# Seven half-size products for the output layer of groups 1 to 8, instead of groups 6 to 8 only

## The chip, the core and the metric

The kernel runs on one core of a Trainium2 chip. The metric is device time in microseconds, from the start of the program on the core to its end; lower is better. The core has five engines that run side by side, each through its own instructions in order: PE (TensorE, matrix products; its weight loads are shown as PEld), DVE (VectorE), ACT (ScalarE), POOL (GpSimd) and SP (SyncE, which here only issues DMAs). They wait for each other through semaphores.

## What is computed

Two layers in a row: linear attention with a softmax-like feature map, and a gated feed-forward layer. Batch 8, 8 heads, 576 positions, head size 64, 128 features; the feed-forward layer has 4608 tokens, a width of 512 and 1536 hidden values.

```python
def phi(x):
    proj = np.einsum('bhsd,df->bhsf', x, w_phi)
    proj = proj - np.max(np.abs(proj), axis=-1, keepdims=True)
    return np.concatenate([np.exp(proj), np.exp(-proj)], axis=-1)
q_p, k_p = phi(q), phi(k)
kv = np.einsum('bhsf,bhsd->bhfd', k_p, v)
z = np.sum(k_p, axis=2)
num = np.einsum('bhsf,bhfd->bhsd', q_p, kv)
den = np.einsum('bhsf,bhf->bhs', q_p, z)[..., None] + 1e-06
x = (num / den)             # tokens x 512 after the heads are put together
gate = np.maximum(x @ w_gate, 0.0)
val = x @ w_val
out = gate * val @ w_out
```

## The kernel before

**Groups.** The 4608 tokens are nine groups of 512. Groups 0 to 7 are the first 512 positions of each batch; group 8 holds the last 64 positions of all eight batches. A group has four blocks of 128 tokens (index t or i), and the hidden layer twelve blocks of 128 values (index f).

**An order written out.** The string ORDER lists some two thousand steps, and the kernel walks through it. A word such as `fv.1.3:0@val3` is a call of `do_fv` for group 1, block 3, on PSUM bank 0, and `@` gives the room of a ring of buffers that a new tile takes. Each engine runs its own steps in the order of this string; a step waits for the steps whose results or rooms it needs. Nothing else plans the work.

**Steps of the attention.** `kt`, `ku`, `qt` transpose k and q (DVE). `kr` (PE, L572) and `qc` (PE, L834) form the projections, `ke` and `qe` their exponentials (ACT, L668 and L849), `kx` and `qx` the maxima (DVE), `kk` the scale of k (ACT). `vs` and `vq` scale v with it (POOL, L725 and L753). `kv` is the product of features and v (PE, L774), `nu` that of q's features with it (PE, L897); `mc`, `mn` are the same for group 8. `nt`, `nv`, `nr` and `nx` normalize (DVE three times, L918, L928 and L936, then POOL, L940), and `xt` turns the result into the layout xT for the next layer with a DMA on SP's queue. `lk`, `lq`, `lm`, `ln` are loads that POOL issues, `lv` and `lw` those of SP.

**Steps of the feed-forward layer.** `fv` and `fg` are the value and gate products of one hidden block (PE, L1074, four products of 512 columns). `va` (ACT) or `vb` (DVE) copies the value from PSUM, `ga` (DVE, L1095) makes h = max(gate, 0) x value in bf16. Group 0 is done in smaller pieces (`pv`, `pg`).

**The output in groups 0 to 5.** `fo.g.t.part` is a third of out[t] = h[:, t] times w_out (PE, L1135, twelve products of 512 columns for a block t, 48 for a group). `oc` (ACT) or `oe` (DVE) copies the bank into one of three buffers ob, and `od` (SP) writes it out.

**The output in groups 6 to 8** is computed by the Winograd form of Strassen's product. h is cut in halves by tokens (r) and by hidden blocks (c), w_out by hidden blocks and by columns; seven products of half size take the place of eight, with sums around them:

- `tw.n.hf` (POOL, L1223): the four differences of blocks of w_out, once for all groups, each in two parts. They lie in the rooms of kn, qn and kT, which are free late.
- `ps.g.n.j` (POOL, L1240): the four sums of blocks of h, n = 1 to 4, for each of six hidden blocks j; 128 x 256 each. Sums 1 and 2 are followed by those that read them.
- `fw.g.n` (PE, L1264): product n, twelve products of 256 columns. Product 5 reads sum 1, 6 reads sum 2, 7 reads sum 3, 3 reads sum 4; 1, 2 and 4 read h itself.
- `ys`, `y2` (ACT) copy banks; `yw`, `yz`, `y1`, `y3`, `y4` (DVE, L1295) add banks into the output in SBUF. The last four quarters come out of these.
- `ow`, `oq` (SP) and `oz` (ACT's queue) write out. `ow` of group 8 is two DMAs, since its blocks hold two batches.

The sums take rooms of the ring vs (four), h takes the ring h2 (15 rooms), and in groups 7 and 8 the rooms of kp.

Of the kernel before, what the change touches and what calls it, by code (L numbers as in the profile page):

```python
# [8 lines left out]
FP32 = mybir.dt.float32  # L9
# [67 lines left out]
fo.0.3.2:1 ln.1.1 lw.2.1 qc.2.0:2456 kt.3.0@kT3 ke.2.2.0.1:3 fv.1.3:0 kx.2.2.3:7 vs.2.0.1@vs0
qx.2.0.3:6 qx.2.0.0:2 oc.0.3:1@ob0 kk.2.1.1 fv.1.4:1 qe.2.0.1.0:4@qp2 vb.1.4:1@val0 vs.2.1.0@vs3
qe.2.0.1.1:4 ke.2.2.0.0:3 kk.2.2.0@ek1 qx.2.0.2:5 kk.2.2.1 qe.2.0.3.1:6@qp3 fg.1.3:7 qe.2.0.3.0:6
vb.1.3:0@val3 fv.1.5:3 lw.3.0 fv.1.1:1 qe.2.0.0.1:2@qp4 fv.1.6:6 qe.2.0.2.1:5@qp0 qt.2.1@qT2  # L80
fg.1.4:0 vb.1.1:1@val2 va.1.5:3@val1 qe.2.0.0.0:2 vs.2.2.1@vs1 ga.1.3:7@hs12 qx.2.0.1:4 qe.2.0.2.0:5
va.1.6:6@val3 qc.2.1:3215 ga.1.4:0@hs13 mn.0.1:7 qe.2.1.2.1:1 fg.1.6:4 ku.3 qe.2.1.3.1:5 qx.2.1.1:2
qe.2.1.0.0:3 fv.1.8:6 nt.8.0.1:7@t1 vs.2.1.1 qx.2.1.3:5 qe.2.1.2.0:1 fg.1.5:0 qx.2.1.0:3
qe.2.1.3.0:5 qx.2.1.2:1 qe.2.1.1.0:2 fv.1.10:5 vq.2.1 qe.2.1.0.1:3 ga.1.5:0@hs14 va.1.8:6@val0
fg.1.0:1 nv.8.0.1:7 vs.2.0.0 lw.3.1 va.1.10:5@val1 ga.1.6:4@hs0 od.0.2 qe.2.1.1.1:2 kr.3.0:3076
lm.4.1 fv.1.0:5 kx.3.0.0:3@mk3 ke.3.0.2.1:7@kp2 lq.3.2 ke.3.0.3.1:6 kx.3.0.1:0 qy.2.0:4 ke.3.0.0.0:3
fg.1.8:2 qz.2.0:4@my0 ke.3.0.1.1:0 vs.2.2.0 kt.3.1@kT2 va.1.0:5@val3 kv.2.0:4 kx.3.0.2:7
ke.3.0.1.0:0 kv.2.1:5 ke.3.0.0.1:3 qu.2.0@mz1 ga.1.8:2@hs1 lm.4.0 lv.3.1 qw.2.0@cq0 ke.3.0.3.0:6
# [48 lines left out]
nt.8.1.0:1@t2 qe.4.0.1.0:4 qc.4.1:5732 kd.4.1:0@kv1 vs.4.2.0 fo.2.1.0:6 qe.4.1.0.1:5 qx.4.1.3:2
# [129 lines left out]
def kernel(  # L267
# [11 lines left out]
    nc = tc.nc  # L279
# [1093 lines left out]
```

## Time and profile before

| | us |
|---|---|
| median of 3 runs | 371.83 (371.48 to 373.03) |
| the profiled execution's own time | 371.23 |
| its span (first to last instruction) | 369.4 |
| HBM read / written | 37.81 MB / 9.44 MB |

The granted clock of TensorE is full speed in every slice of the span. "Busy" is the union of the intervals in which an engine had an instruction; short overlaps of neighbours count once. "x48" is a number of instructions. The chain of work that ended last is followed back from the last instruction, at each step to what released it. In stretches, the columns are the length, then for PE, PEld, DVE, ACT and POOL the busy time and the number of instructions, then the clock, the DMA share and GB/s. Lines L... are lines of the kernel. In the groups, out<-in stands for the tile written and those read, and the numbers behind the bar are the busy time in us and the mean of one in ns, then the idle time of the engine ahead of it with what ended it.

### The profile page before, as it was taken

The numbers are of one execution on the slowest core, as the hardware profiler recorded it, in microseconds if no ns is written. First come the engines' busy times: TensorE is split into PE (matmuls) and PEld (weight loads), VectorE is DVE, ScalarE is ACT, GpSimd is POOL, SyncE is SP. The second block draws the span as 40 slices with busy tenths as digits, with TensorE's granted clock in tenths as the row PEclk, the third lists the DMA queues.
The fourth block names the chain that finished last, engine by engine and source line by source line (L and its number), as shares of the span: only waits on it lengthen the run. The fifth ranks groups of instructions, "written<-read, shape, count | busy, mean of one in ns | idle before, by whom it ended". The sixth has DMA issues, their size and how long they took to land.

```text
span 369.4 us, 9471 instructions
## 1 busy us (share of the span) xinstructions
PE 359.6 (97%) x3672; PEld 206.1 (56%) x3720; DVE 292.9 (79%) x682; ACT 228.1 (62%) x552; POOL 215.1 (58%) x241
## 2 busy tenths in 40 slices
PE   8999999999999999999999999999999999999995
PEld 6579865446544654464465444654445684444674
DVE  6999999999989999999888797777558775347433
ACT  4999996998588855986775539735656402312110
POOL 8675995293379049713760438367078972285690
PEclk9999999999999999999999999999999999999999
DMA  8999999909657983493356061835020010700007
GB/s 132 248 206 196 174 196 144 184 26 164 108 127 113 170 135 76 71 186 78 80 114 105 14 116 57 138 83 118 0 59 1 2 27 14 232 0 3 0 18 212
DMA packets 90767, 38.13 MB, mean 103 GB/s; under 512 B 64226, under 2 KB 86370, under 8 KB 90722
## 3 DMA queue, kind: packets, MB, share of 16 engines
q0 software_dynamic: 33504, 15.03, 30.9%
q1 hardware_dynamic: 57074, 22.36, 26.6%
q8 instruction: 29, 0.48, 0.5%
q14 instruction: 16, 0.13, 0.1%
q10 hardware_dynamic: 144, 0.13, 0.1%
HBM read 37.81 MB, written 9.44 MB: 128 GB/s over the span
## 4 chain that ended last, share of the span: by engine, by line
PE 82%; POOL 7%; DVE 5%; DMA 3%; issue 2%; ACT 0%; POOLq 0%; DVEq 0%
PE bank L1074 42%; PE bank L1135 16%; PE bank L1264 6%; PE bank L774 4%; PE bank L1103 4%; POOL vs L1240 4%; PE bank L897 4%; DMA vn<-in_v_dram 3%; PE bank L572 2%; PE bank L834 2%; DVE h L1095 2%; DVE mk L676 1%; POOL vs L725 1%; DVE t L918 1%; PE bank L1053 1%
## 5 line engine op out<-in xcount | busy, mean ns | idle before, releaser
L668 ACT ACTIVATE kp<-bank 128x384 bf16<-128x384 f32 x192 | 84.4, 517 | 20.0 <-PE bank L572 13.1
L1089 ACT CAST val<-bank 128x512 bf16<-128x512 f32 x81 | 47.2, 595 | 65.3 <-PE bank L1074 44.4
L1074 PE MATMUL bank<-xTs,wv 128*128 128x512 bf16 x338 | 86.0, 379 | 0.7
L1074 PE MATMUL bank<-xTs,wg 128*128 128x512 bf16 x335 | 85.2, 379 | 0.9
L940 POOL TENSOR_TENSOR xu<-u,r 128x512 bf16<-128x512 f32 x36 | 37.3, 1042 | 71.6 <-DVE r L936 51.6
L849 ACT ACTIVATE qp<-bank 128x512 bf16<-128x512 f32 x128 | 70.0, 621 | 11.6 <-PE bank L834 9.9
L1135 PE MATMUL bank<-wo,h 128*128 128x512 bf16 x274 | 66.1, 379 | 0.7 <-issue 0.2
L725 POOL TENSOR_TENSOR vs<-vn,ek 128x780 bf16<-128x780 f32 (+2 forms) x40 | 53.7, 1365 | 21.4 <-ACT ek L685 13.5
L1074 PEld LDWEIGHTS <-wg 128*128 128x128 bf16 x400 | 37.5, 98 | 40.7
L1095 DVE SCALAR_TENSOR_TENSOR h<-bank,val 128x512 bf16<-128x512 f32 x76 | 51.0, 679 | 11.5 <-PE bank L1074 8.8
L1074 PEld LDWEIGHTS <-wv 128*128 128x128 bf16 x400 | 37.1, 98 | 41.2 <-issue 1.5
L676 DVE TENSOR_REDUCE mk<-bank 128x3 f32<-128x384 f32 x96 | 50.1, 541 | 5.3 <-ACT kp L668 3.3
L1135 PEld LDWEIGHTS <-h 128*128 128x128 bf16 x288 | 26.4, 98 | 31.2 <-issue 2.4
L857 DVE TRANSPOSE_TENSOR_REDUCE maxq<-bank 128x16 f32<-128x512 f32 x56 | 37.2, 691 | 3.9 <-ACT qp L849 2.0
L928 DVE TENSOR_TENSOR u<-bank,t 128x195 f32<-128x195 f32 (+1 forms) x108 | 33.5, 329 | 3.0 <-POOL xu L940 1.2
L918 DVE TENSOR_TENSOR t<-bank,cq 128x195 f32<-128x195 f32 (+1 forms) x96 | 30.0, 325 | 3.3 <-PE bank L897 3.1
L897 PEld LDWEIGHTS <-qp 128*128 128x128 bf16 x512 | 23.0, 98 | 11.2 <-issue 1.9
L1095 DVE SCALAR_TENSOR_TENSOR kp<-bank,val 128x512 bf16<-128x512 f32 x24 | 16.1, 688 | 14.9 <-PE bank L1074 13.1
L897 PE MATMUL bank<-kv,qp 128*128 128x65 bf16 x512 | 25.8, 193 | 0.3 <-ACT kv L785 0.2
L774 PEld LDWEIGHTS <-kp 128*128 128x128 bf16 x640 | 21.5, 97 | 3.2 <-issue 0.7
L774 PE MATMUL bank<-vs,kp 128*128 128x65 bf16 x512 | 22.1, 193 | 0.4 <-POOL vs L725 0.4
L753 POOL TENSOR_TENSOR vr<-vm,ek 64x520 bf16<-64x520 f32 x14 | 14.8, 1060 | 11.0 <-DMA vm<-in_v_dram 9.6
(129 smaller groups left out, 492.7 us busy)
## 6 DMA issues: line engine op xcount, KB each, us to landing
vn<-in_v_dram SPq DMA_DIRECT2D x24, 256.0 KB, 4.9
out_dram<-ob SPq DMA_DIRECT2D x24, 256.0 KB, 3.1
kn<-in_k_dram POOLq DMA_DIRECT2D x7, 512.0 KB, 9.5
qn<-in_q_dram POOLq DMA_DIRECT2D x7, 512.0 KB, 7.5
wv<-in_moe_w_val_dram POOLq DMA_DIRECT2D x3, 512.0 KB, 9.6
wg<-in_moe_w_gate_dram POOLq DMA_DIRECT2D x3, 512.0 KB, 9.1
wo<-in_moe_w_out_dram POOLq DMA_DIRECT2D x3, 512.0 KB, 8.1
out_dram<-xTs SPq DMA_DIRECT2D x5, 256.0 KB, 2.6
```

What stands on the lines that cost most here:

```text
L668: nc.scalar.activation(kp_of(3 * b + j)[:, i, s].rearrange("p n f -> p (n f)"), bank[bk[0]][:, 0 : 3 * F], AF.Exp, scale=(1.0, -1.0)[s],)
L676: nc.vector.tensor_reduce(mk_of(3 * b + j)[:, :, i], bank[bk[0]][:, 0 : 3 * F].rearrange("p (n f) -> p n f", f=F), axis=AX.X, op=ALU.max, ...
L725: nc.gpsimd.tensor_tensor(vs_of(3 * b + j)[:, s, 0:n].rearrange("p n i e -> p (n i) e")[:, :, 0:e], src[:, lo:hi].rearrange("p h i e -> p ...
L774: nc.tensor.matmul(out_ps[:, h - lo, s, :], lhsT=lhsT, rhs=rhs, start=(at == 0), stop=(at == 2 * n * (C + 1) - 1),)
L849: nc.scalar.activation(qp_of(4 * b + i)[:, s, 4 * hq : 4 * hq + 4].rearrange("p h m -> p (h m)"), bank[bk[0]], AF.Exp, scale=(1.0, -1.0)[s],)
L857: nc.vector.tensor_reduce((maxq0[:, i] if b == 0 else maxq)[:, :, i, 4 * hq : 4 * hq + 4].rearrange("p t h -> p h t"), bank[bk[0]].rearran ...
L897: nc.tensor.matmul(bank[bk[0]][:, E * n : E * (n + 1)], lhsT=qp_of(4 * b + i)[:, s, h, :], rhs=kv_of(b)[:, h, s, 0:E],)
L940: eng.tensor_tensor(xu_of(n).rearrange("p (h d) -> p h d", d=D), u_of(n)[:, :, 0:D], r_of(n).to_broadcast([P, H, D]), op=ALU.mult,)
L1074: nc.tensor.matmul(bank[bk[0]], lhsT=w[:, dc, P * f : P * f + P], rhs=xT(g)[:, dc, :], start=(dc == 0), stop=(dc == NDC - 1),)
L1089: nc.scalar.copy(val_of(NFC * g + f), bank[bk[0]])
L1095: nc.vector.scalar_tensor_tensor(h2_of(g, f), bank[bk[0]], 0.0, val_of(NFC * g + f), op0=ALU.max, op1=ALU.mult)
L1135: nc.tensor.matmul(bank[bk[0]], lhsT=h2_of(g, f)[:, P * t : P * t + P], rhs=wo_sb[:, f, :], start=(f == 0), stop=(f == NFC - 1),)
```

## The change

- Groups 1 to 5 take the seven half-size products as well. Their `fo`, `oc`, `oe` and `od` words are gone; `fw`, `ps`, `ys`, `y...` and `ow` words stand in their place. Group 0 keeps `fo`, and all its four copies are `oc` on ACT.
- The three ob buffers become one pair. Group 0's four output blocks have four rooms: two in its own xT room and the pair. In later groups the first half of the output goes into the group's own xT room and the second into the pair (group 7: the xT room of group 6).
- The differences of w_out are made early, right after group 0's output, and stay: the first in place over the block of w_out that no later product reads, the second and third in room kp3, the fourth in room qp0. So kp has three rooms and qp four for the rest.
- Sums 3 and 4 of h are written over the blocks of h that they replace. vs has five rooms, h2 sixteen; group 8's h lies in h2.
- 18 sums, 12 of group 7 and 6 of group 8, are made by DVE (new step `ds`, function of the same formula) instead of POOL.
- From the word `oc.0.1` on the whole of ORDER is in another sequence. Ahead of it nothing differs.

```diff
-    vs_of = ring("vs", 4, [P, 2, 3, 4, EP], BF16)
+    vs_of = ring("vs", 5, [P, 2, 3, 4, EP], BF16)
-    ob_of = ring("ob", 3, [P, DM], FP32)
+    ob_pair = sb.tile([P, 2, DM], FP32, name="obp", tag="obp")
-    NH2 = 15
+    NH2 = 16
...
     def do_oc(bk, g, t):
-        nc.scalar.copy(ob_of(4 * g + t), bank[bk[0]])
+        nc.scalar.copy(ow_pair(g, t // 2)[:, t % 2], bank[bk[0]])
...
-    WG = (6, 8, 7)
+    WG = tuple(range(1, B + 1))
...
+    def tw_all(n):
+
+        if n == 0:
+            return wo_sb[:, 0:HK, HN:DM]
+        if n == 3:
+            return flat_of(qp_of(("tw",)).rearrange("p s h m -> p (s h m)"), HK)
+        t = kp_of(("tw",)).rearrange("p i s n f -> p (i s n f)")
+        return flat_of(t[:, HK * HN * (n - 1) : HK * HN * n], HK)
...
-    def sum_of(g, n):
+    def sum_of(g, n, j):
+
+        if n > 2:
+            return h_block(g, 1, 0, j) if n == 3 else h_block(g, 0, 1, j)
         t = vs_of(("sum", g, n)).rearrange("p s n i e -> p (s n i e)")
-        return flat_of(t, HK)
+        return flat_of(t, HK)[:, j]
...
     def ow_pair(g, r):
 
-        room = {6: (xT_all[:, 0], xT_all[:, 1]), 8: (xT_all[:, 0], xT_all[:, 1])}.get(
-            g, (xT_all[:, 2], xT_mix)
-        )[r]
+        if r == 1 and g != B - 1:
+            return ob_pair
+        room = xT(g) if r == 0 else xT_all[:, 2]
```

Of the new sequence, two stretches of which the prediction speaks: the one around group 2's first kv, with the differences of w_out in front, and the end.

```
oc.0.0:4 kr.2.2:3054 ku.3@kT3 qt.2.0@qT0 xt.1.1 ke.2.1.0.1:7 xt.1.0 tw.1.0 ke.2.1.3.0:6 ln.1.1
...
ke.2.2.0.1:3 kk.2.0.0 qc.2.0:6401 fv.1.3:2 fv.1.10:3 od.0.1 oc.0.3:7 tw.0.0 qe.2.0.1.0:4@qp2 tw.0.1
...
qc.2.1:7650 od.0.2 qe.2.1.2.0:5 fg.1.6:1 qe.2.1.0.0:7 va.1.11:2@val3 qx.2.1.1:6 fg.1.11:4 vs.2.1.0
kt.3.0 qx.2.1.0:7 kv.2.1:3 vs.2.2.0@vs0 qe.2.1.1.1:6 qe.2.1.0.1:7 qt.3.1@qT1 vs.2.2.1 od.0.3 tw.2.1
...
ds.7.4.3 y1.7.1:5 fw.8.4:1 y3.8:1 ow.8.2 ow.8.3 ps.8.4.2 ds.7.4.4 ps.8.4.4 fw.7.5.0:2 ps.8.4.3
ps.8.4.0 fw.7.4:3 y1.7.0:2 oq.7.1.1 fw.8.3:0 y3.7:3 oq.7.1.0 fw.7.3.1:5 fw.7.3.0:2 y4.8:0 y4.7.1:5
y2.8:6 ow.8.0 ow.8.1 oz.7.1 y4.7.0:2 ow.7.0.1
```

The words by kind, before and after: fo 72 and 12, oc 16 and 4, oe 8 and 0, od 24 and 4, fw 23 and 58 (four of them half steps), ps 72 and 174, ds 0 and 18, ow 9 and 29, ys 3 and 8, y2 3 and 8, yw, yz and y3 3 and 8 each, y1 and y4 4 and 9 each.

More of the change, by code (lines that the diff above doesn't have):

```diff
@@ new lines @@
+qe.3.0.1.0:7 qe.3.0.2.0:4 kk.3.2.1@ek4 kk.3.0.1 fw.1.7:0 yz.1:0 ps.1.4.0 qe.3.0.3.0:2@qp4
+qc.3.1:3674 qx.3.1.3:4 qx.3.1.0:3 vs.3.1.0@vs4 ps.1.4.3 lq.4.2 xt.2.2 kk.3.2.0 vq.3.0@vr0 ps.1.4.2
+qe.3.0.3.1:2 fw.1.4:0 vq.3.1 vs.3.1.1 vs.3.2.0@vs0 qe.3.1.3.1:4 qe.3.1.3.0:4 kt.4.1@kT2 vs.3.2.1
+qe.3.1.1.1:6 fv.2.10:2 qe.3.0.0.1:1@qp1 y3.1:0 fv.2.2:4 fg.2.1:0 qx.3.1.1:6 va.2.10:2@val0
+qe.3.1.0.1:3 qe.3.1.1.0:6 fv.2.1:2 qx.3.0.0:1 qx.3.1.2:7 ps.1.4.1 fg.2.2:6 kt.4.0 vb.2.2:4@val2
+ps.1.4.5 qe.3.1.0.0:3 y1.1:5 qe.3.0.0.0:1 qy.3.0:3 qz.3.0:3@my1 kv.3.1:1 qu.3.0@mz0 fv.2.11:4
@@ new lines @@
+qt.5.1@qT0 va.3.11:6@val2 nx.4.0@xu3 nv.4.1.0:5 fv.3.10:6 fg.3.1:5 ga.3.11:7@hs9 va.3.1:2@val3
+nr.4.1@r1 nt.4.3.1:4@t2 vs.5.0.1@vs2 kx.5.1.3:0 ps.3.1.5 nt.4.3.0:3@t1 fg.3.4:7 nu.4.3.2:2
+kx.5.1.2:1 ke.5.1.2.1:1 nv.4.3.1:4@u0 ga.3.1:5@hs8 nv.4.3.0:3 va.3.10:6@val1 nt.4.3.2:2@t3
+kr.5.2:0415 xt.8.0 ga.3.4:7@hs2 nu.4.2.1:6 fv.3.7:3 ke.5.2.2.1:1@kp2 nv.4.3.2:2 nr.4.3@r2
+ke.5.2.0.0:0 fg.3.7:7 kx.5.2.2:1@mk5 nu.4.2.2:2 va.3.7:3@val2 ke.5.2.3.1:5 vq.5.1@vr0 ow.2.2
+nt.4.2.1:6@t0 fg.3.10:3 ga.3.7:7@hs0 ke.5.2.2.0:1 nx.4.1@xu0 fv.3.8:1 nt.4.2.2:2@t2 xt.4.1
@@ new lines @@
+nt.5.0.2:0@t0 kk.6.0.1 fv.4.9:3 y4.3:2 nt.5.0.1:1@t2 ow.3.3 nv.5.0.2:0 nu.5.1.2:4 fv.4.2:6
+nv.5.0.1:1 nu.5.1.0:2 nt.5.1.2:4@t1 nr.5.0@r2 vq.6.0@vr1 nx.5.0@xu3 lw.6.1 va.4.9:3@val2 fg.4.9:3
+nv.5.1.2:4@u1 nu.5.3.0:0 xt.5.0 nt.5.1.0:2@t3 nu.5.3.1:1 nt.5.3.1:1@t0 nt.5.3.0:0@t2 my.2:4
+va.4.2:6@val0 mz.2:4@my2 fg.4.4:6 ke.6.0.0.1:5 nv.5.3.0:0@u2 fv.4.0:5 ga.4.9:3@hs11 nu.5.1.1:4
+nu.5.2.0:0 ga.4.4:6@hs5 fv.4.6:3 ps.4.1.1@vs1 nt.5.2.0:0@t1 fv.4.8:6 nv.5.1.0:2 nt.5.1.1:4@t2
+nv.5.1.1:4 vb.4.0:5@val2 nu.5.3.2:2 nu.5.2.2:4 fv.4.3:5 nv.5.3.1:1 va.4.3:5@val1 nr.5.1@r1 lv.6.0
@@ new lines @@
+ke.7.2.1.1:0 fv.5.11:6 fw.5.1:2 ps.5.3.3 ke.7.2.0.0:3 ke.7.2.1.0:0 va.5.11:6@val0 ps.5.1.2
+ga.5.6:7@hs3 ke.7.2.3.0:5 kk.7.1.1@ek4 ps.5.1.1 ys.5:2 ps.5.1.0 fg.5.11:1 kx.7.2.2:4 kx.7.2.0:3
+qc.7.0:7063 xt.6.2 kx.7.2.3:5 kk.7.2.0@ek2 vq.7.0@vr0 ke.7.2.2.1:4 kk.7.1.0 ga.5.11:1@hs12
+qx.7.0.1:0 qe.7.0.1.1:0@qp4 qt.7.1@qT2 ps.5.2.0 xt.6.1 qx.7.0.2:6 fw.5.2:2 vs.7.1.1@vs2 xt.6.0
+fv.6.0:5 fg.6.0:1 va.6.0:5@val1 ga.6.0:1@hs14 qe.7.0.1.0:0 y2.5:2 fv.6.4:5 fv.6.1:0 ps.5.4.0
+va.6.4:5@val2 fv.6.10:1 ps.5.3.0 ke.7.2.2.0:4 va.6.1:0@val3 fg.6.4:2 qe.7.0.2.0:6@qp3 fv.6.3:5
@@ L1064, in h2_of @@
         i = NFC * g + f
-        if g >= B - 1:
+        if g == B - 1:
             t = kp_of(("h", g, f // 6)).rearrange("p i s n f -> p (i s n f)")
@@ L1143, in do_oc @@
     def do_oc(bk, g, t):
-        nc.scalar.copy(ob_of(4 * g + t), bank[bk[0]])
+        nc.scalar.copy(ow_pair(g, t // 2)[:, t % 2], bank[bk[0]])
     def do_oe(bk, g, t):
-        nc.vector.tensor_copy(ob_of(4 * g + t), bank[bk[0]])
+        nc.vector.tensor_copy(ow_pair(g, t // 2)[:, t % 2], bank[bk[0]])
     def do_od(bk, g, t):
@@ L1153, in do_od @@
                 dst = out[0:SF, :].rearrange("(p c) n -> p c n", c=C)[:, t]
-            nc.sync.dma_start(out=dst, in_=ob_of(4 * g + t))
+            nc.sync.dma_start(out=dst, in_=ow_pair(g, t // 2)[:, t % 2])
             return
@@ L1158, in do_od @@
             nc.sync.dma_start(
-                out=out[r0 : r0 + SM, :], in_=ob_of(4 * g + t)[SM * bb : SM * (bb + 1)]
+                out=out[r0 : r0 + SM, :], in_=ow_pair(g, t // 2)[:, t % 2][SM * bb : SM * (bb + 1)]
             )
-    HD = DM // 2
-    def do_fp(bk, g, t, half):
-        for f in range(NFC):
-            nc.tensor.matmul(
-                bank[bk[0]][:, 0:HD],
-                lhsT=h2_of(g, f)[:, P * t : P * t + P],
-                rhs=wo_sb[:, f, HD * half : HD * (half + 1)],
-                start=(f == 0),
-                stop=(f == NFC - 1),
-            )
-    def do_o1(bk, g, t):
-        nc.scalar.copy(ob_of(4 * g + t)[:, 0:HD], bank[bk[0]][:, 0:HD])
-    def do_o2(bk, g, t):
-        nc.vector.tensor_copy(ob_of(4 * g + t)[:, HD:DM], bank[bk[0]][:, 0:HD])
-    def do_d1(bk, g, t):
-        r0 = S * g + P * t
-        nc.scalar.dma_start(out=out[r0 : r0 + P, 0:HD], in_=ob_of(4 * g + t)[:, 0:HD])
-    def do_d2(bk, g, t):
-        r0 = S * g + P * t
-        nc.sync.dma_start(out=out[r0 : r0 + P, HD:DM], in_=ob_of(4 * g + t)[:, HD:DM])
-    WG = (6, 8, 7)
+    WG = tuple(range(1, B + 1))
     HK = NFC // 2
@@ L1257, in do_fw @@
                 else:
-                    x = sum_of(g, {3: 4, 5: 1, 6: 2, 7: 3}[n])[:, j]
+                    x = sum_of(g, {3: 4, 5: 1, 6: 2, 7: 3}[n], j)
                 if n in (1, 2, 3):
```

392 lines of the change are left out of this document (180 added, 212 removed).

## The prediction, made before the changed kernel was run

> **What bounds the kernel now.** I read the page first: its first lines, then the chain of work that ended last.
>
> ```profile
> span 369.4 us, 9471 instructions
> PE 359.6 (97%) x3672; PEld 206.1 (56%) x3720; DVE 292.9 (79%) x682; ACT 228.1 (62%) x552; POOL 215.1 (58%) x241
> ...
> PE 82%; POOL 7%; DVE 5%; DMA 3%; issue 2%; ACT 0%; POOLq 0%; DVEq 0%
> ```
>
> PE is busy nearly all the time and carries 82% of the chain. Busy PE need not be PE at its peak, so I looked at how densely its products start. These are pieces of the chain (start, us, what): a run of h times w_out the old way (L1135, 512 columns) and one as half-size products (L1264, 256 columns), with the first layer and small products beside them.
>
> ```profile
> 302.06 1.31 PE bank L1264 x12
> 102.78 4.32 PE bank L1135 x20
> 305.26 10.74 PE bank L1074 x49
> 101.81 0.56 PE bank L834 x8
> 144.41 0.63 PE bank L1053 x32
> ```
>
> A 512-column product takes 4.32/20 = 0.216 us, a 256-column product 1.31/12 = 0.109 us: 1% dearer per column than the long one. In the middle nothing but the number of columns sets PE's time. The stretches show where the other engines stand (stretch, us, busy us of PE, PEld, DVE, ACT, POOL; clock):
>
> ```profile
> 45.00:70.00 25.00, 24.68 (x357) 14.60 (x362) 24.68 (x70) 21.52 (x60) 16.91 (x20) 1.00 1.31 180
> 70.00:100.00 30.00, 29.73 (x336) 15.69 (x340) 28.56 (x63) 25.71 (x63) 15.37 (x15) 1.00 0.68 106
> 100.00:130.00 30.00, 29.68 (x299) 15.02 (x302) 27.14 (x63) 24.34 (x60) 16.27 (x15) 1.00 0.74 134
> 250.00:280.00 30.00, 29.79 (x207) 13.55 (x210) 19.26 (x34) 17.30 (x42) 16.12 (x14) 1.00 0.24 54
> ```
>
> The reader is to see that DVE is almost as full as PE between 45 and 130 us and half idle late, while POOL has room throughout. From 45 to 70 both PE and DVE are 99% busy, so a full DVE does not by itself hold PE up.
>
> **What the change removes and adds.** Groups 1 to 5 now compute their output in seven products of halves. Per group 48 products of 512 columns (12 steps fo) go, and 84 of 256 (seven steps fw) come: 48 x 0.216 = 10.37 us against 84 x 0.109 = 9.17 us, so 1.2 us less, for five groups **6.0 us less on PE**. PE is the bound where this happens, so it counts in full unless something makes PE wait.
>
> [...]
>
> The sums, copies and differences that go with the products:
>
> ```profile
> L1240 POOL TENSOR_TENSOR vs<-h 128x256 bf16<-128x256 bf16 x12 | 8.0, 673 | 1.5 <-DVE h L1095 1.4
> L1223 POOL TENSOR_TENSOR kT<-wo 128x768 bf16<-128x768 bf16 x2 | 3.3, 1636 | 0.0
> L1295 DVE TENSOR_TENSOR xTs<-bank,xTs 128x512 f32<-128x512 f32 x10 | 6.9, 688 | 4.4 <-ACT xTs L1289 2.5 <-PE bank L1264 1.8
> L1295 DVE TENSOR_TENSOR xTs<-bank,xTs 128x256 f32<-128x256 f32 x2 | 0.8, 425 | 0.2 <-PE bank L1264 0.2
> L1144 ACT COPY ob<-bank 128x512 f32<-128x512 f32 x16 | 9.5, 595 | 12.0 <-PE bank L1135 11.9
> L1147 DVE COPY ob<-bank 128x512 f32<-128x512 f32 x8 | 5.4, 677 | 3.7 <-PE bank L1135 3.6
> L936 DVE RECIPROCAL r<-u 128x8 f32<-128x8 f32 x36 | 6.8, 192 | 0.5
> ```
>
> POOL: 24 sums per group for five groups are 120, of which the order hands 18 of groups 7 and 8 to DVE: 102 x 0.67 = 68 us more, 215 to 283 us. DVE: five adds per group of 0.69 us, 25 x 0.69 = 17 us, less the eight copies oe (5.4 us). The 18 late sums on DVE have no row: above the reciprocal on 8 columns (0.19) and, without waits, at most the add on 256 columns (0.43). I take 0.43, the row of their size, 8 us. That makes DVE about 313 us. ACT: 16 copies go, 4 of group 0 and 10 new ones come, about nothing. All of this lies beside PE's work as long as sums arrive in time; that is the question.
>
> The eight differences of w_out (tw) cost the same as before but move to the front: 8 x 1.64 = 13 us of POOL before group 2's v products, and lm, lq, vq, vs stand behind them in POOL's queue. Here I sum the tightest chain. From the end of fo.0.3.0 (which frees the block that tw.0.0 overwrites) to vs.2.1.0, which kv.2.1 waits for, POOL has four tw (6.6), the DMA issues lm and lq, two vq and two vs:
>
> ```profile
> L725 POOL TENSOR_TENSOR vs<-vn,ek 128x780 bf16<-128x780 f32 x24 | 35.6, 1499 | 12.8 <-ACT ek L685 12.7
> L753 POOL TENSOR_TENSOR vr<-vm,ek 64x520 bf16<-64x520 f32 x14 | 14.8, 1060 | 11.0 <-DMA vm<-in_v_dram 9.6 <-ACT ek L685 0.9
> L488 POOL DMA_DIRECT2D km<-in_k_dram x14 | 10.3, 738 | 2.4 <-DVE u L928 2.4
> L476 POOL DMA_DIRECT2D qn<-in_q_dram x9 | 8.0, 893 | 12.2 <-DVE qT L825 10.8 <-PE bank L802 1.4
> L940 POOL TENSOR_TENSOR xu<-u,r 128x512 bf16<-128x512 f32 x36 | 37.3, 1042 | 71.6 <-DVE r L936 51.6 <-issue 19.3 <-PE bank L897 0.7
> ```
>
> 6.6 + 0.7 + 0.9 + 2 x 1.06 + 2 x 1.50 = 13.3 us. PE meanwhile has thirteen blocks of four 512-column products (13 x 0.86), two qc (0.56 each) and the mn (0.6): 12.9 us. The second chain is nx.2.2 to vs.3.1.1, for kv.3.1: 1.04 + seven sums (4.7) + 0.9 + 2.1 + 3.0 = 11.7 us; PE has five fw (6.6), five blocks (4.3) and two qc (1.1), 12.0 us, less what nt, nv and nr take on DVE before nx.2.2 can start, about 0.9 (0.35, 0.35, 0.19 in their rows):
>
> ```profile
> L928 DVE TENSOR_TENSOR u<-bank,t 128x195 f32<-128x195 f32 x72 | 24.7, 353 | 2.1 <-POOL xu L940 0.8
> L918 DVE TENSOR_TENSOR t<-bank,cq 128x195 f32<-128x195 f32 x64 | 21.8, 346 | 2.5 <-PE bank L897 2.4
> ```
>
> Both chains come out short by about half a microsecond with these means; back to back the sums are a little quicker (three in 1.89 us, below) and small PE steps are left out, so I call them even and take 0.3 us of new waits. Bounds: none, or, if all of POOL's excess lands on PE, the slower rival below.
>
> **What goes.** PE waits now for POOL's sums in groups 6 and 7. From the timeline, with the waits in brackets, and the chain before the first of them:
>
> ```profile
> 289.51 1.89 POOL vs L1240 x3
> ...
> 295.96 0.28 PE L1264 MATMUL bank<-qn,vs 128*128 128x256 bf16 x1 [0.28 <-POOL vs L1240]
> 296.59 0.61 PE L1264 MATMUL bank<-qn,vs 128*128 128x256 bf16 x4 [0.34 <-POOL vs L1240]
> ...
> 354.71 1.57 PE L1264 MATMUL bank<-qn,vs 128*128 128x256 bf16 x12 [0.42 <-POOL vs L1240]
> ```
>
> That is 1.0 us. In the new order group 6's sums are spread out, and in group 7 only eight POOL sums lie between the last h and the end of sum 2: 8 x 0.63 = 5.0 us, with some 1.5 us for the value copy and ga ahead of them, against five fw (6.6 us) on PE. I take 1.0 us as gone.
>
> **What is late next: the tail.** In the old order the output of group 8 leaves before the end. The new one puts y3.8, four DMAs, two oq, y4.8, four more DMAs and then ow.7.0.1, the last, on SP's queue. SP's and ACT's issues at the end, and the time to landing of L1317's:
>
> ```profile
> 358.23 5.32 SPq L1321 DMA_DIRECT2D out_dram<-xTs  x8
> 363.65 0.53 SPq L1325 DMA_DIRECT2D out_dram<-xTs  x1
> 363.97 1.47 PE L1264 MATMUL bank<-wo,vs 128*128 128x256 bf16 x12
> 365.94 0.37 ACTq L1332 DMA_DIRECT2D out_dram<-xTs  x1
> DMA to landing us min/median/max: 2.4/2.8/3.0
> ```
>
> Call the end of the last product T (now 363.97 + 1.47 = 365.4; the span ends 4.0 later). In the new order fw.8.4 ends 4.6 before T (3.5 fw follow). DVE has an add and two shorter pieces in front, so y3.8 is done near T - 3.5. SP: four issues (5.32 for eight: 2.7 us) to T - 0.8, two oq (0.53 each) to T + 0.3, y4.8 is long done, four issues to T + 2.9, ow.7.0.1 lands 2.8 later at T + 5.7, and from a landing to the span's end it is now 1.0 us (365.94 + 2.5 to 369.4, with 2.5 the landing of that one). T + 6.7 against T + 4.0: **2.6 us more**, or 0 at best, if the issues are hidden after all.
>
> Four rooms for group 0's output, fewer rooms for kp and qp, and outputs written into a group's own xT room cost nothing in this sum: SP issues as many outputs per group as before, and ACT, which fills kp and qp, is 62% busy. If that cover fails, kv's next group waits for a room; I bound it by the chain of POOL below.
>
> **The sum.** The profiled execution took 371.23 us, its span 369.4; the median of the runs shown is 371.83, 0.6 above it. 371.23 - 6.0 - 1.0 + 2.6 + 0.3 = 367.1; on the median's scale **367.7 us**.
>
> **The rivals.**
> - *The tail is hidden* (the last issues overlap, as in the old order): 367.7 - 2.6 = 365.1. Against it: a queue issues in order and the eight took 5.32 us. Chance 0.13.
> - *DVE is late.* It idles 4.3 us between 70 and 130; two groups' adds (6.9) less two oe (1.4) want 5.5. The missing 1.2 and some 0.6 at each of the two chains are 2.4 us of PE waits: 370.1. For it: DVE's rows; against it: 45 to 70. Chance 0.20, half of it above the bound of faster.
> - [...] Chance 0.07.
> - *POOL becomes the bound: slower.* From kr.2.1 to vs.3.0.0 the order gives POOL 25 sums (16.8), seven tw (11.5), six nx (6.3), four vq (4.2), twelve vs (16.2) and ten DMA issues (8), 63 us, and PE 40 blocks (34.5), seven fw (9.2) and some 12 us of small products, 56 us. If DVE delays nx or ga so that POOL cannot work ahead, PE waits for all of it: 7 more, 374.7. It decides from 4.1 us of added waits. For it: both chains are even at best; against it: POOL's idle time before tw. Chance 0.09.
> - *The products are no cheaper* than rows say: nothing speaks for it. Chance 0.01.
>
> **Chances.** The forecast, 366 to 369, has 0.50. A measurement of this kernel tells about 0.5% from no change, so faster means below 370.0: 0.50 + 0.13 + 0.07 + half of 0.20 = 0.80. Within 0.5%: the other half and a bit of the slower rival, 0.12. Slower: 0.08. For 8 in 10 the range takes the forecast, the lock, most of late DVE and the edge of the hidden tail: 365.2 to 371.0.
>
> **What would show it.** The 512-column products with w_out fall to 48 and those of 256 columns rise to 672, still at 0.109 us; DVE is 97% busy or more between 70 and 130; the waits of PE for vs stay below 1 us each; the last event is an SP DMA issued some 3 us after the last product. Wrong if PE waits for vs before kv.2.1, kv.3.1 or kv.3.0, if DVE is the longest piece of the chain in the middle, or if the time after the last product stays near 4 us.

## The result and the profile after

The changed kernel takes 367.70 us (median of 4 runs, 367.59 to 367.82), the kernel before took 371.65 us (371.19 to 373.03) in the runs beside it: a ratio of 0.9888 (95% interval 0.9861 to 0.9914), 1.1% faster. The forecast was 367.7 us. Its profiled execution took 367.77 us, where the one of before took 371.23: 3.5 us less, and the sum of the forecast, made against that execution, said 4.1.

The first lines of the page and the shares of the chain of work that ended last, after the change:

```profile
span 365.9 us, 9975 instructions
PE 355.0 (97%) x3853; PEld 224.7 (61%) x3900; DVE 307.4 (84%) x717; ACT 228.6 (62%) x550; POOL 279.9 (77%) x343
...
PE 82%; DVE 9%; POOL 4%; issue 2%; ACT 1%; DVEq 0%; POOLq 0%
```

PE is as full as before and has as large a share of the chain. POOL got 64.8 us more (215.1 to 279.9), DVE 14.5 (292.9 to 307.4). The stretches show where that lies (stretch, us, then busy us of PE, PEld, DVE, ACT, POOL; clock, DMA share, GB/s):

```profile
45.00:70.00 25.00, 24.51 (x338) 14.28 (x343) 24.67 (x68) 21.16 (x57) 22.54 (x25) 1.00 1.36 169
70.00:100.00 30.00, 29.72 (x339) 15.96 (x343) 28.56 (x67) 22.87 (x58) 29.72 (x30) 1.00 0.68 120
100.00:130.00 30.00, 29.56 (x364) 19.12 (x369) 29.55 (x70) 24.81 (x63) 29.58 (x36) 1.00 0.72 114
250.00:280.00 30.00, 29.79 (x233) 16.69 (x236) 22.23 (x39) 20.74 (x49) 21.82 (x27) 1.00 0.09 23
```

From 70 to 130 us POOL went from 53% to 99% busy. Three engines are full there, and the busy shares alone cannot say which of them sets the pace. In the chain (start, us, what) POOL carries the stretch ahead of group 2's products:

```profile
121.78 0.98 PE bank L1081 x4
...
125.52 1.05 POOL vr L760
126.65 0.67 POOL vs L1223
...
133.23 1.89 POOL vs L1223 x3
...
141.33 0.68 POOL vs L1223
142.05 2.58 PE bank L1247 x22
...
342.62 17.09 PE bank L1247 x156
```

The reader is to see that the chain goes over POOL for 16 us, sums (L1223) and normalizations with short gaps between them, and that from 342.62 it stays on half-size products: 156 in 17.09 us, 0.110 us each. The products of 512 columns with w_out are 48 now (group 0 alone). The waits for the sums of groups 6 and 7 (0.28, 0.34 and 0.42 us before) are not in this trace.

The end, from the timeline (start, us, SPq and ACTq are issues of DMAs):

```profile
355.87 2.49 SPq L1304 DMA_DIRECT2D out_dram<-obp  x4
358.22 1.47 PE L1247 MATMUL bank<-wo,kp 128*128 128x256 bf16 x12
358.46 1.07 SPq L1308 DMA_DIRECT2D out_dram<-xTs  x2
359.53 0.37 ACTq L1315 DMA_DIRECT2D out_dram<-xTs  x1
359.63 2.70 SPq L1304 DMA_DIRECT2D out_dram<-xTm  x4
362.42 0.53 SPq L1300 DMA_DIRECT2D out_dram<-xTs  x1
```

The last product starts at 358.22 instead of 363.97 us, **5.75 us earlier**. From there to the span's end it is 7.7 instead of 5.4 us: **2.2 us given back**. The issues stand as forecast, ow.7.0.1 last, 2.7 us after the last product ended (359.69). Whether they are the cause was a question for the chip.

The late sums on DVE, from the groups by shape and the timeline:

```profile
L1223 DVE TENSOR_TENSOR kp<-kp 128x256 bf16<-128x256 bf16 x6 | 3.4, 584 | 0.8 <-POOL vs L1223 0.8
L1223 DVE TENSOR_TENSOR kp<-kp,vs 128x256 bf16<-128x256 bf16 x6 | 2.9, 508 | 0.0
L1223 DVE TENSOR_TENSOR h<-h 128x256 bf16<-128x256 bf16 x6 | 2.1, 357 | 0.0
...
341.60 0.28 DVE L1223 TENSOR_TENSOR h<-h 128x256 bf16<-128x256 bf16 x1
344.74 2.09 DVE L1223 TENSOR_TENSOR kp<-kp 128x256 bf16<-128x256 bf16 x3 [0.78 <-POOL vs L1223]
```

A sum takes 0.28 us on DVE when POOL makes none, and 0.70 us (2.09/3) in the row that lies beside POOL's sums. One by one, ten of the 18 took 0.28 us, seven of them without a sum on POOL, and eight, all beside POOL's sums, 0.69 to 0.76.

### The profile page after: what moved, and what is told of

The parts are those of the page before. It is cut to its first block, busy times and chain, and to the rows that moved or that the text cites. A ratio compares the mean times of both kernels' runs of the same rounds, so it can differ in the third digit from the quotient of the medians.

```text
span 365.9 us, 9975 instructions
## 1 busy us (share of the span) xinstructions
PE 355.0 (97%) x3853; PEld 224.7 (61%) x3900; DVE 307.4 (84%) x717; ACT 228.6 (62%) x550; POOL 279.9 (77%) x343
## 4 chain that ended last, share of the span: by engine, by line
PE 82%; DVE 9%; POOL 4%; issue 2%; ACT 1%; DVEq 0%; POOLq 0%
PE bank L1081 41%; PE bank L1247 18%; PE bank L781 4%; PE bank L1110 4%; PE bank L904 3%; PE bank L442 2%; PE bank L1142 2%; PE bank L841 2%; PE bank L579 2%; POOL vs L1223 2%; DVE t L925 2%; DVE h L1102 1%; DVE u L935 1%; ACT kp L675 1%; DVE mk L683 1%
## 5 line engine op out<-in xcount | busy, mean ns | idle before, releaser
L1102 DVE SCALAR_TENSOR_TENSOR h<-bank,val 128x512 bf16<-128x512 f32 x88 | 59.1, 681 | 20.0 <-PE bank L1081 12.3
L683 DVE TENSOR_REDUCE mk<-bank 128x3 f32<-128x384 f32 x96 | 49.2, 543 | 1.2 <-ACT kp L675 0.9
L1223 POOL TENSOR_TENSOR vs<-h 128x256 bf16<-128x256 bf16 x42 | 27.9, 669 | 28.8 <-DVE h L1102 23.3
L1247 PEld LDWEIGHTS <-h 128*128 128x128 bf16 x420 | 39.9, 98 | 9.3 <-issue 2.4
L1247 PE MATMUL bank<-wo,h 128*128 128x256 bf16 x252 | 31.0, 273 | 0.1
L1223 POOL TENSOR_TENSOR vs<-vs,h 128x256 bf16<-128x256 bf16 x42 | 27.7, 669 | 0.9 <-PE bank L1247 0.2
L1223 POOL TENSOR_TENSOR h<-h,vs 128x256 bf16<-128x256 bf16 x42 | 27.8, 676 | 0.0
L1223 POOL TENSOR_TENSOR h<-h 128x256 bf16<-128x256 bf16 x36 | 23.7, 669 | 0.3
```

The source lines that it names most:

```text
L683: nc.vector.tensor_reduce(mk_of(3 * b + j)[:, :, i], bank[bk[0]][:, 0 : 3 * F].rearrange("p (n f) -> p n f", f=F), axis=AX.X, op=ALU.max, ...
L1102: nc.vector.scalar_tensor_tensor(h2_of(g, f), bank[bk[0]], 0.0, val_of(NFC * g + f), op0=ALU.max, op1=ALU.mult)
L1223: eng.tensor_tensor(sum_of(g, n, j), a, b, op=op)
L1247: nc.tensor.matmul(bank[bk[0]][:, col : col + HN], lhsT=x[:, P * u : P * (u + 1)], rhs=w, start=(n in (1, 5, 6) and u == us[0] and j == 0) ...
```

## The experiments

Twelve kernels, each built from the changed one. Theory: PE sets the pace nearly everywhere, so the gain is its columns; POOL's chains are just even; the end is an order of issue. Rivals: POOL or DVE sets the pace from 60 to 140 us; the end is the transfers themselves; the late sums or the rooms decide. Times are medians and stand against 367.70 us; t1_tail and r3_rooms came out without effect and so show, at 367.68 and 367.56, that this mark held beside the runs measured with them (z1_at130, z2_at323 and g5_fo; t2_ports, p1_pool and d1_pool). Beside t3_queues and n1_half, and beside b1_tail and b2_casts, there is no such run; the kernel before took 371.28 and 371.61 us there, against 371.35 to 371.65 elsewhere, so a few tenths of a microsecond between their medians and 367.70 say little by themselves.

### Does PE set the pace? (z1_at130, z2_at323)

```
-fg.2.9:6
+zz.28:6 fg.2.9:6        (z1_at130)
-fw.6.3:5
+zz.28:5 fw.6.3:5        (z2_at323)
```

In z2_at323 the zeros overwrite a partial result of group 6 in bank 5; the work is the same.

> The changed kernel with 28 more products of zeros (128x256, 0.109 us each, 3.05 us together) ahead of fg.2.9, at about 130 us, whose result nobody reads. There GpSimd is busy for 99% and VectorE for 95% of the time. Theory (TensorE sets the pace in this stage too, GpSimd and VectorE are only just even with it): +2.3 to +3.1 us, 370.0 to 370.8. Rival (GpSimd and VectorE set the pace between 60 and 140 us, TensorE waits for them): the zeros fill waits, +0 to +1.2 us, at most 368.9.

> The same 28 products of zeros (3.05 us), ahead of fw.6.3 at about 323 us. Theory (TensorE sets the pace from here to the end): +3.05 us, 370.6 to 370.9. Rival (the sums of groups 7 and 8 on VectorE and GpSimd set the pace of the last 25 us): +0 to +1.2 us, at most 368.9.

Measured: 370.91 us (370.39 to 372.76) and 370.91 us (370.70 to 372.18), both 3.2 us more, where the zeros are 3.05. What PE was given came out at the end, in the stage where POOL and DVE are full as well as in the late one. The theory holds in both, a little above its ranges. The stretch 130 to 140 us of the changed kernel, and then of z1_at130, where the zeros ran from 129.9 to 133 us:

```profile
130.00:140.00 10.00, 9.90 (x111) 5.49 (x101) 8.91 (x24) 7.94 (x18) 9.92 (x15) 1.00 0.57 105
130.00:140.00 10.00, 9.89 (x89) 6.12 (x91) 6.32 (x17) 5.37 (x12) 7.30 (x11) 1.00 0.56 105
```

While the zeros ran, DVE was busy for 6.32 us and POOL for 7.30, each 2.6 us less than without them: they stood still until PE went on. They did not work ahead; the sums read h, and h is made from PE's products. In this one traced execution the last product moved by 2.5 us (360.72) and the span by 2.9 (368.8). But its first product with w_out, ahead of which the two programs are alike, starts at 56.76 instead of 57.06 us. Counted from there the last product moved by 2.8 us, so at most some 0.25 us of PE's waits had been there for the zeros to fill.

### Had POOL anything to spare? (p1_pool, n1_half)

```
-ps.2.1.4
+ps.2.1.4 ps.2.1.4 ps.2.1.4 ps.2.1.4        (p1_pool)
-ps.1.3.0 … ps.5.4.5   (all 60 sums 3 and 4 of groups 1 to 5)        (n1_half)
```

> The changed kernel with one sum on GpSimd (ps.2.1.4) done four times instead of once, 1.9 to 2.0 us more of GpSimd at about 127 us, where its chain of sums and normalizations ends level with TensorE's need. Theory (that chain is even with TensorE, with a few tenths to spare at most): +0.8 to +1.9 us, 368.5 to 369.6. Rival (GpSimd has 2 us or more to spare behind TensorE): within 0.3 us of 367.7. Second rival (GpSimd sets the pace there already): all of it, +1.9 to +2.2 us.

> The changed kernel without the third and fourth sums of groups 1 to 5 (60 of the 120 sums on GpSimd, 40 us of it); the products that read them read the unsummed blocks instead, so that these groups' outputs differ, and TensorE's work is the same. Theory (the prediction's missing microsecond, 5.75 us gained at the last product where 6.7 were forecast, is TensorE waiting in many small places for GpSimd's sums): -0.7 to -1.5 us, 366.2 to 367.0. Rival (it is not the sums; VectorE or the banks hold TensorE up): within 0.4 us of 367.7.

Measured: 369.90 us for p1_pool, 2.2 us more, and 367.28 us (366.99 to 367.60) for n1_half, 0.4 us less. The traces agree: their first products with w_out start at 57.10 us in n1_half and 57.06 in the changed kernel, the last ones at 357.81 and 358.22. The page of n1_half has this row:

```profile
PE 356.4 (98%) x3900; PEld 224.3 (61%) x3900; DVE 307.3 (84%) x717; ACT 228.5 (63%) x550; POOL 242.6 (66%) x283
```

The larger share of PE must not be read as waits that are gone. This trace has all 3900 products, that of the changed kernel 3853 beside 3900 weight loads, and a missing record looks like idle time: from 310 to 340 us, where the two kernels are alike, PE is busy for 30.00 us here and 29.84 there.

Together the two runs say how the engines stand. All of POOL's 1.9 us more came through: nothing to spare, the second rival. But half of its sums taken away brought only 0.4 us. So the chain on POOL and the one on PE are of the same length there, within a few tenths; more on either lengthens the run, less on POOL alone hardly shortens it. The waits for sums 3 and 4 cost 0.4 us, less than the theory gave them: the larger part of the missing microsecond is not there.

### Is the gain its columns? (g5_fo)

```
-fw.5.1 ys.5 fw.5.2 y2.5 fw.5.6 yw.5 fw.5.7 yz.5 fw.5.4 fw.5.5 y1.5 y3.5 fw.5.3 y4.5, ps.5.n.j
+fo.5.t.part (12 steps), oc.5.t
+        if g == 5 and f in (0, 1, 2, 3, 5):
+            ... h in the rooms of vs that the sums had
```

The steps fo of group 5 read a block of w_out that tw.0 has replaced by a difference, so this group's output differs.

> The changed kernel with group 5 as before: 48 products of 512 columns (12 steps fo.5, placed where the seven products of group 5 stood) instead of 84 of 256; its 24 sums on GpSimd, two copies and five additions are gone, four copies come back. Five blocks of its hidden layer lie in the rooms that its sums had. Theory (the change's gain is its columns): +1.2 us (48 x 0.216 - 84 x 0.109), 368.9, and the sums that go (24 x 0.67 = 16 us of GpSimd, two thirds of them beside a busy TensorE) bring nothing. Rival (the sums hold up TensorE and eat most of the gain): between -0.5 and +0.4 us, at most 368.1.

Measured: 368.76 us (368.30 to 369.57), 1.1 us more. The first product with w_out and the last product, from PE's timelines of the changed kernel (the first of them) and of g5_fo:

```profile
57.06 1.02 PE L1142 MATMUL bank<-wo,h 128*128 128x512 bf16 x4
```

```profile
56.72 1.03 PE L1134 MATMUL bank<-wo,h 128*128 128x512 bf16 x4
...
359.04 1.47 PE L1239 MATMUL bank<-wo,kp 128*128 128x256 bf16 x12
```

The last product comes 0.8 us later (359.04 against 358.22). But this execution was 0.34 us ahead at the first product with w_out, where the two programs do not yet differ; counted from there it is 1.16 us. The theory holds against the rival: the sums do not eat the gain. Group 5 gives 1.1 to 1.2 us, as 48 x 0.216 - 84 x 0.109 says. It stands where POOL and DVE have room (250 to 280 us); for groups 1 and 2, where they have none, this was not tried.

### What are the late sums on VectorE worth? (d1_pool)

```
-ds.g.n.j
+ps.g.n.j        (18 sums)
```

> The changed kernel with all 18 late sums (ds, groups 7 and 8) on GpSimd instead of VectorE. GpSimd was busy for 15.8 of the 25 us from 330 to 355 us and gets 18 x 0.67 = 12.1 us more, VectorE loses 18 x 0.28 to 0.70. Theory (late sums on VectorE are what keeps the last 25 us on TensorE): 28 us of work in 25, +2 to +5 us, 369.7 to 372.7. Rival (they bring nothing, GpSimd would have been ready): within 0.5 us of 367.7.

Measured: 370.32 us, 2.6 us more. PE's timeline in d1_pool, with the wait in brackets:

```profile
351.93 1.16 PE L1237 MATMUL bank<-kp,vs 128*128 128x256 bf16 x9 [2.27 <-POOL vs L1213]
```

One wait of 2.27 us for a sum on POOL is nearly all of it. The theory held: with the late sums on POOL, two thirds of the gain would be gone.

### Four rooms or three? (r3_rooms)

```
+    def first_room(g, t):
+        return ow_pair(0, 0)[:, 1] if (g, t) == (0, 3) else ow_pair(g, t // 2)[:, t % 2]
```

> The changed kernel with three rooms instead of four for the first group's output: the block of t=3 takes the room of t=1, so its copy on ScalarE (oc.0.3) waits until the DMA of t=1, issued just before, has landed, some 2.5 us at about 74 us, with the exponentials of q of batch 2 queued behind it. Theory (ScalarE is covered there; the fourth room is worth little): +0 to +0.5 us, 367.7 to 368.2. Rival (the wait comes through to TensorE by the banks that the exponentials empty): +1.2 to +2.5 us, 368.9 to 370.2.

Measured: 367.56 us (367.45 to 368.27), nothing. The wait does not come through, and the fourth room is worth nothing measurable.

### What sets the end? (t1_tail, t2_ports, t3_queues, b1_tail)

First the order of issue:

```
-ow.8.0 ow.8.1 oz.7.1 y4.7.0 ow.7.0.1
+ow.8.0 oz.7.1 ov.8.1 y4.7.0 ow.7.0.1        (ov: as ow, on nc.scalar's queue)
```

> The changed kernel with one output block of group 8 (ow.8.1, two DMAs) issued from ScalarE's queue, behind oz.7.1, instead of SyncE's; nothing else differs. Theory (the end is set by the order of issue: SyncE needs 0.63 to 0.68 us for each of the four DMAs of L1304 that stand ahead of ow.7.0.1, so that its issue starts 2.7 us after the last product began to be read out): with two of the four gone, ow.7.0.1 is issued at about 361.0 instead of 362.42 us and the time falls by 1.4 us, from 367.7 to about 366.3. Rival (the last landing takes as long whatever the order, since the transfers of 0.25 MB themselves fill the time): within 0.4 us of 367.7.

Measured: 367.68 us (367.63 to 367.91), no change. The issue did move, and the end did not. The timeline of t1_tail, then a group of its DMAs by issue (count, KB each, median us to landing):

```profile
360.96 1.13 SPq L1290 DMA_DIRECT2D out_dram<-xTs  x1
...
out_dram<-xTs SPq DMA_DIRECT2D x1, 128.0 KB, 3.8
```

ow.7.0.1 was issued 1.5 us earlier, took 1.13 instead of 0.53 us to issue and landed 3.8 instead of 2.5 us after. **So the theory that the prediction used for the tail is wrong**: not the queue but the transfers fill the end. Stretches of the changed kernel's end agree with it (the last but one number is the share of the 16 DMA engines):

```profile
358.50:360.50 2.00, 1.20 (x11) 0.82 (x9) 1.43 (x3) 0.00 (x0) 0.00 (x0) 1.00 0.97 255
360.50:363.00 2.50, 0.00 (x0) 0.00 (x0) 0.00 (x0) 0.00 (x0) 0.00 (x0) 1.00 1.01 294
```

From 358.5 to 363 us the DMA engines have no time left (0.97 and 1.01). Before the change group 8's DMAs began 5.7 us ahead of the last product's start (358.23 against 363.97), now they begin 2.4 us ahead (355.87 against 358.22): the bytes are the same, and they start later. The suspects were the transfers of group 8, 1.0 of the last 1.75 MB, each from 64 partitions.

```
+            dst = out.rearrange("(b s) n -> b s n", s=S)[2 * t : 2 * t + 2, SF:S, :]
+            nc.sync.dma_start(out=dst, in_=src)        (t2_ports: one DMA for both batches)
```

> The changed kernel with each block of group 8's output written by one DMA of 128 partitions (0.25 MB, both batches' rows) instead of two of 64 partitions (0.125 MB each); four such blocks stand in the tail. Theory A (after t1_tail: the end is set by the transfers of the last 1.75 MB, and those from 64 partitions move at about 205 GB/s where those from 128 partitions moved at 332 to 347 GB/s): each of the two pairs of blocks takes 1.5 instead of 2.5 us, and the time falls by 1 to 2 us, to 365.7 to 366.7. Theory B (the transfers into memory have one rate whatever their partitions, or their receipt sets the end): within 0.4 us of 367.7, as t1_tail.

Measured: 385.08 us, 17.4 us more, which neither theory said. The timeline of t2_ports and, from 340 to 384 us in slices of 1.1 us, the DMA engines' share in tenths and their GB/s:

```profile
361.51 6.94 SPq L1304 DMA_DIRECT2D out_dram<-xTm  x2
...
DMA  0000000001500000112796111111112311111000
GB/s 0 0 0 0 0 15 0 0 0 62 176 0 0 0 0 11 30 26 63 192 301 163 52 52 48 52 48 48 41 52 79 123 55 52 50 50 52 26 0 0
```

In the slices from 364 to 381 us, all but three (41, 79 and 123 GB/s), it is a tenth of the DMA engines' time at about 50 GB/s. What makes one DMA over both batches so slow is not shown. The run thus says nothing of the partitions, and they were tried in another way.

```
+            queue = (nc.sync, nc.scalar)[bb]
+            queue.dma_start(out=out[r0 : r0 + SM, cols], in_=src[SM * bb : SM * (bb + 1)])
```

> The changed kernel with group 8's output as eight DMAs of 64 partitions as before, but those of the upper 64 partitions issued from ScalarE's queue, so that both halves of the partitions are under way at once; the blocks and their sizes are the same. [...] Theory B (the memory or the receipts set the end): within 0.4 us of 367.7.

Measured: 367.02 us (366.68 to 367.11), 0.7 us less. GB/s from 339 to 366 us in slices of 0.675 us, of the changed kernel (first) and of t3_queues (second):

```profile
GB/s 0 0 0 0 0 0 0 0 0 0 24 0 0 0 0 0 0 212 176 0 0 0 0 0 0 0 49 209 206 203 223 338 358 232 250 331 216 103 0 0
```

```profile
GB/s 0 0 0 0 0 0 0 0 0 0 24 0 0 0 0 0 0 241 147 0 0 0 0 0 0 0 76 231 349 282 326 335 300 288 291 231 9 0 0 0
```

With one queue the first four DMAs, of 64 partitions each, move at 203 to 209 GB/s, and the rate rises to 338 only when those of 128 partitions follow. SP's pace of issue, 128 KB every 0.62 us, would by itself allow no more than 211 GB/s. That it is the transfers shows in the share of the DMA engines (last but one number; the changed kernel):

```profile
358.46:359.63 1.17, 1.17 (x12) 0.86 (x9) 1.04 (x2) 0.00 (x0) 0.00 (x0) 1.00 0.98 201
359.63:362.40 2.77, 0.07 (x1) 0.00 (x0) 0.42 (x1) 0.00 (x0) 0.00 (x0) 1.00 0.99 288
```

As good as all of the engines' time goes into 201 GB/s first and into 288 later. With the halves on two queues the rate stays near 300 (282 to 349 in seven slices). The gain of 0.7 us lies above theory B's 0.4. It is less than the whole difference of the rates: by an estimate from them, 0.5 MB for a pair of blocks take 2.5 us at 205 GB/s and 1.5 us at the 332 to 347 of the stores of 128 partitions at the end of the kernel before (365.3 to 368 us), 1.0 us less for each of the two pairs. In the traced execution, the fastest of four, the end comes 6.6 us after the last product's start (358.16) instead of 7.7. How much of the 0.7 us comes from sharing the time of issue between two queues is not separated from the transfers.

Last, fewer bytes at the end:

```
-y2.7:7 oq.7.0.0 … y1.8:0 … ow.8.2 ow.8.3 … y2.8:6 ow.8.0 ow.8.1
+y2.7:7 y2.8:6 ow.8.0.0 ow.8.1.0 oq.7.0.0 … y1.8:0 ow.8.2.1 ow.8.3.1 … ow.8.2.0 ow.8.3.0 … ow.8.0.1 ow.8.1.1
```

> As t3_queues, and each block of group 8's output is sent as two halves of 256 columns, each as soon as its last addition is done: the first halves of t=0 and t=1 already after y2.8 (copied at about 350 us) and the second halves of t=2 and t=3 after y1.8 (about 353 us), when the DMAs stand still, so that 0.5 instead of 0.75 MB are left to send after 359 us. Theory (the end is set by the transfers that are left when the last product is done): 0.4 to 1.0 us less than t3_queues' 367.0, 366.0 to 366.6. Rival (what is left is issue and receipt of ow.7.0.1, 3.2 us after its issue whatever is under way): within 0.3 us of 367.0.

Measured: **365.59 us** (365.33 to 365.78), 1.4 us less than t3_queues, where the theory gave at most 1.0, and 2.1 us less than the changed kernel; against the kernel before a ratio of 0.9846 (0.9832 to 0.9861). From its trace, the last issues and the time behind the last product:

```profile
359.94 0.54 SPq L1290 DMA_DIRECT2D out_dram<-xTs  x1
360.24 0.55 ACTq L1306 DMA_DIRECT2D out_dram<-xTs  x1
```

```profile
360.50:362.00 1.50, 0.00 (x0) 0.00 (x0) 0.00 (x0) 0.00 (x0) 0.00 (x0) 1.00 0.94 265
362.00:363.40 1.40, 0.00 (x0) 0.00 (x0) 0.00 (x0) 0.00 (x0) 0.00 (x0) 1.00 0.00 0
```

The DMA engines are done at 362 us now, where the changed kernel kept them busy until about 364, and ow.7.0.1 lands 2.2 us after its issue, instead of 2.5 there and 3.8 in t1_tail. From the last product's start to the span's end it is 363.4 - 357.82 = 5.6 us, nearly what it was before the change (5.4). 0.4 us of its gain stand already at the last product (357.82 against 358.22). 0.33 of that were there before the two programs differ: the first product with w_out starts at 56.73 instead of 57.06. That part belongs to this one execution and not to the change at the tail.

### Is DVE what holds PE up? (b2_casts)

```
-vb.g.f        (the eight of groups 1 to 4, on DVE)
+va.g.f        (on ACT)
```

> As b1_tail, and the eight copies of the value layer that VectorE did in groups 1 to 4 (vb) are done by ScalarE (va): 8 x 0.6 = 4.8 us less of VectorE where it is busy for 95 to 99%. Theory (of the 0.95 us that is missing at the last product, the 0.5 that n1_half did not give back is TensorE held up by VectorE): 0.3 to 0.8 us less than b1_tail. Rival (VectorE is covered; the seven products themselves gain less than 6.0 us): within 0.2 us of b1_tail; a third outcome is that ScalarE, 90 to 95% busy from 95 to 110 us, becomes late: more than b1_tail.

Measured: 366.19 us (365.85 to 366.47), 0.6 us more than b1_tail: the third outcome. From 70 to 100 us, b1_tail and then b2_casts:

```profile
70.00:100.00 30.00, 29.73 (x342) 16.09 (x345) 28.57 (x69) 22.79 (x57) 29.71 (x31) 1.00 0.66 115
```

```profile
70.00:100.00 30.00, 29.16 (x334) 15.38 (x337) 26.14 (x62) 23.71 (x60) 29.67 (x30) 1.00 0.75 125
```

DVE lost 2.4 us of work and PE lost 0.57 us of its busy time in that stretch; PE's list of waits has there one of 0.3 us for a value copy on ACT and one of 0.3 us for xTs, which b1_tail has not. The work that left DVE made ACT late, and so this run does not answer the question: whether DVE holds PE up stays open.

## Why the prediction came out as it did

- **PE bound, products of 0.216 and 0.109 us: right.** 156 products in 17.09 us are 0.110 each; the zeros came through in full early and late (3.2 us for 3.05), and g5_fo lost 1.1 us by going back.
- **6.0 us less on PE: right where it was tried.** Group 5 alone gives 1.1 to 1.2 us (g5_fo), a fifth of it.
- **0.3 us of new waits: the mis-sized term.** That POOL's chains and PE's are even was right: p1_pool found nothing to spare. But with 1.0 us of waits gone and 0.3 added the last product should have come 6.7 us earlier, and it came 5.75. If groups 1 to 4 gain on PE what group 5 does, some 1.2 us were lost there and not 0.3. The waits for sums 3 and 4 are 0.4 us of it (n1_half). PE's list of waits has two new ones for DVE of 0.2 us each (nu for u, fw for obp), which n1_half has too. The rest, some half a microsecond, stands in pieces too short for that list, and its cause stays open.
- **1.0 us of waits of groups 6 and 7 gone: right**, they are not in the trace, and d1_pool shows what the late sums on DVE have to do with it.
- **Tail, 2.6 us more: the size nearly right (2.2), the reason wrong.** The prediction read the end from the queue of issues on SP. t1_tail moved the last issue by 1.5 us and gained nothing. The end is 1.75 MB that leave in the last 10 us, 1.0 of them from 64 partitions, of which the first half moved at 203 to 209 GB/s. Spread over two queues and over time (t3_queues, b1_tail), they give the 2.1 us back.
- **POOL 283, DVE 313 us: measured 279.9 and 307.4.** The late sums took 8.4 us where 8 were put in, but not as 18 x 0.43: ten at 0.28, eight at 0.69 to 0.76.
- **The rivals.** Late DVE and POOL as the bound did not come with the prices that they were given, yet p1_pool shows how near the second was: POOL has nothing left from 126 to 142 us (busy for 15.77 of 16). Of the signs of being wrong none came, but the chain has POOL as its longest piece there, which no sign provided for. The lock that the range counts is a term that no run shows as such: what the trace shows is eight late sums of 0.69 to 0.76 us, all beside sums on POOL, against ten of 0.28, and no wait for them in PE's list, since DVE is not late then.
- **The total.** On the profile's scale the sum was 0.7 us too low (367.1 against 367.77): 0.95 us too much gain up to the last product, 0.35 too much loss at the tail. That the median agreed to the tenth is luck: the two errors have opposite signs, and what they left was made up by the step of 0.6 us from execution to median, taken from before, which did not recur (367.77 and 367.70).

## What to carry to other kernels

Price a change on the bounding engine by its instructions, and try it in one place alone (here group 5 gave the 1.2 us reckoned, while the whole came out 0.95 us short). Compare traces from a point ahead of the first difference: here their starts alone differ by 0.3 us. Where two engines are both full, add work to each in turn: a busy share does not tell which one sets the pace, and here either did. At a kernel's end count the bytes that are left, and read from a trace at what rate each form of transfer leaves (here 203 to 209 GB/s from 64 partitions on one queue, about 50 for one DMA over two batches), before counting issues; send what is final early (1.4 us less here), and try two queues for halves (0.7 us less here).

## What the runs showed of the hardware

- A sum of two bf16 tiles of 128x256 on VectorE took 0.28 us in ten cases of 18, seven of them without a sum on GpSimd, and 0.69 to 0.76 us in eight, all beside GpSimd's sums, which then took 0.71 to 0.78 instead of 0.67 us.
- One DMA of 256 KB over two batches moved at about 50 GB/s, with a tenth of the DMA engines' time taken; blocks of the same size as two DMAs moved at 203 to 209 GB/s.
- DMAs of 64 partitions from one queue moved at 203 to 209 GB/s, with 98% of the DMA engines' time taken; when stores of 128 partitions joined them the rate rose to 358. Halves from two queues, stores of 128 partitions among them, moved at 282 to 349.
